# A new written order for a fused attention and highway kernel: same operations, other order, other buffers, other holds of the q loads

## The chip, the cores and the metric

The kernel runs on one core of one Trainium2 chip. The metric is the device time of one execution in microseconds (us). The core has engines that each work through their own list of instructions in order and meet only through semaphores: TensorE (PE in the profile; PEld are its weight loads), VectorE (DVE), ScalarE (ACT), GpSimd (POOL) and SyncE (SP, which here only issues DMAs). DMAs are issued from the lists of SP, POOL and (four of them) ACT, and are moved by 16 DMA engines that all of them share.

## What is computed

```python
def _attn_ref(q, k, v, tau):           # 8 batches, 12 heads, 448 tokens, 64 wide, float32
    q_n = q / (np.linalg.norm(q, axis=-1, keepdims=True) + 1e-06)
    k_n = k / (np.linalg.norm(k, axis=-1, keepdims=True) + 1e-06)
    scores = np.matmul(q_n, k_n.transpose(0, 1, 3, 2)) / tau
    scores = scores - np.max(scores, axis=-1, keepdims=True)
    attn = np.exp(scores)
    attn = attn / (np.sum(attn, axis=-1, keepdims=True) + 1e-09)
    return np.matmul(attn, v)

def _moe_ref(x, w_h, w_t, b_t):        # x: 3584 tokens x 768
    H = np.maximum(x @ w_h, 0.0)
    T = 1.0 / (1.0 + np.exp(-(x @ w_t + b_t)))
    return T * H + (1.0 - T) * x
```

The attention's output, laid out as 8 * 448 tokens by 12 * 64, is the x of the second part.

## The kernel before

**The work and its names.** Each of the 8 batches goes through the same stages. The names are those of the program's operations; the first number is mostly the batch.

- *Loads.* `ldq b` on SP; `ldk b` and `ldv4`, `ldv3` (quarters of v) on POOL, where k and v turn to 16 bits on the way. Of batch 0, q comes in three loads and k in three (`ldf 0` on ACT, `ldf 1` and `ldf 2` on SP); of batch 1, q comes in three (`ldq 1 0`, `ldq 1 1`, `ldq 1 2`). `ldwt` and `ldwh` (POOL) bring the weights, `ldb` (SP) is three loads of the bias.
- *Norms.* `sq2` squares a group of heads (ACT, some on POOL), `rd2` sums them (DVE), `ln28` and `ie28` (ACT, first two groups of batch 0 and the third) or seven `nt` steps (DVE) make one over the root, `qn7`, `kn4`, `kn3` scale (POOL, first group on DVE too).
- *Turning.* q and k are transposed either by TensorE (`tq`, `tk`, then copies `cpq`, `cpk` on DVE) or by DMA from SP (`xd7` for q from batch 3 on, `xdk` for k from batch 5 on).
- *Attention.* Six pairs of heads per batch, numbered n = 6 b + p. `qk n c` (two products of 64 rows each, L496) and `qkt n` (L507) make scores, `exp` and `expt` (ACT, L502, L509) take them to 16 bits, `av n c` and `avt n` (L521, L526, L534) multiply with v, `rc` and `ev` (DVE) divide and write x. Batch 0 is cut otherwise: `qk01`, `qt01`, `ex512`, `ex384`, `av0`.
- *Second part.* Four blocks per batch, g = 4 b + i. x is turned by DMA (`xd6 g`, `xd3 g` on SP) except in batch 0 (`xt6`, `xt3` on TensorE). `ff g wi half lo` (three products of 128 x 384, L682; `fft`, L679, for the small fourth block) are the products with wt (wi 0) and wh (wi 1). `za` (DVE) adds the bias, `th6` or `th3` (ACT) takes tanh, `gt`, `hm`, `gg` (DVE) and `out` (POOL) combine, `st g` (SP) stores. The last two blocks end in `cx`, `hg6`, `ou6`, `hg3`, `ou3` on DVE and `sl` stores on SP and ACT; the last products are two `fth`.
- *Fillers.* 57 products of zeros (`wm`, `wf`) keep TensorE working in the first 30 us.

**What sets the order.** All 1948 operations stand in one written list, `ORDER`; each engine runs its own in the order of that list. `SLOTS` gives, for each ring of buffers, which buffer the n-th tile to be touched takes (`B` are the eight PSUM banks, `qr` the two buffers of loaded q, `kr` three of k, and so on). A tile may only take a buffer whose former tile is done with, so a load also waits for the last reader of that buffer. Two further sorts of waits are put in by hand at the end of the kernel: an operation on POOL of certain kinds waits for the last one of those kinds on DVE, and the q loads of batch 1 and later (`held`) wait for whatever ACT operation stands last before them in the list. In the list before, these are: `ldq 1 0` the first table load, `ldq 1 2` an `sq1` of group 0, `ldq 1 1` `ln28 0 56`, `ldq 2` `ex384 0 1 0`, `ldq 3` `ex384 1 3 0`, `ldq 4` `th3 3`, `ldq 5` `exp 15 2 0`, `ldq 6` `exp 22 1 0`, `ldq 7` `exp 31 2 0`.

Of the kernel before, what the change touches and what calls it, by code (L numbers as in the profile page):

```python
# [94 lines left out]
""".split()  # L95
)

SLOTS = {
    "qr": "01010101",
    "kr": "0120121",  # L100
    "kn": "012012021012021021021021",
    "vr": "01010101",
    "vp": "01010101",
    "sq": "012012010201210210210210120102102100120210120210",
    "n2": "01010101",
    "y": "01201201",
    "tu": "01010101010",
# [93 lines left out]
def kernel(  # L201
# [609 lines left out]
    with nc.allow_low_precision(reason="fp16 operands of the products and gates as given"):  # L811
        with tc.manual_schedule():
            before = act = None
# [50 lines left out]
```

## Time and profile before

| | us |
|---|---|
| timed runs | 254.82, 256.25, 258.32 (median 256.25) |
| span of the profiled execution, first to last instruction | 252.9 |
| TensorE busy in it | 237.5 |
| ScalarE busy | 211.5 |
| VectorE busy | 208.0 |
| GpSimd busy | 184.0 |

The page gives no other time of the profiled execution than its span; the timed runs count what lies around it too. In the views, a line such as `L682 PE MATMUL B<-wt,xT` is an instruction of line 682 that writes a tile of ring B and reads wt and xT. Busy TensorE is not TensorE at its peak, since products overlap: a product of 384 columns counts as busy for longer than the time after which the next one may start. "From issue to landing" of a DMA counts from the start of its issuing instruction.

### The profile page before, as it was taken

The page shows a single profiled execution, that of the slowest core. Times are in us where ns is not written, and L with a number is a line of the kernel's source. Part 1 is how long each engine was busy: PE and PEld are TensorE (multiplying, and loading weights), DVE is VectorE, ACT ScalarE, POOL GpSimd, SP SyncE. Part 2 cuts the span into 40 slices and gives each one's busy share as a digit, 9 for nine tenths or more (in the row PEclk, how much of TensorE's full clock was granted, in tenths as well). Part 3 has the DMA queues.
Part 4 walks back from the last instruction along what each step waited for, and adds up shares of the span by engine and source line. Part 5 has one row for each costly group of instructions (what it writes and reads, how often), then busy time and mean ns, then how long its engine had stood idle before and what let it go on. Part 6 is the DMA issues. An engine that isn't in the chain of part 4 may idle for free.

```text
span 252.9 us, 7457 instructions
## 1 busy us (share of the span) xinstructions
PE 237.5 (94%) x2895; PEld 147.1 (58%) x2895; DVE 208.0 (82%) x462; ACT 211.5 (84%) x421; POOL 184.0 (73%) x261
## 2 busy tenths in 40 slices
PE   5959999999999999989999999999999999999990
PEld 2425776557756665645765566656656655675650
DVE  4977989999999999989899869689767665556983
ACT  3589999999999999989999999999997669981120
POOL 8369599959798979796989775878476983522540
PEclk9997999999999999999999999999999999999998
DMA  6999999999589999999999998999779588745755
GB/s 219 286 270 237 288 259 202 200 271 179 72 104 146 314 264 248 151 223 163 266 157 170 156 114 138 249 207 193 128 129 231 93 135 192 162 127 123 187 147 156
DMA packets 75892, 47.78 MB, mean 189 GB/s; under 512 B 51536, under 2 KB 72656, under 8 KB 75856
## 3 DMA queue, kind: packets, MB, share of 16 engines
q1 hardware_dynamic: 55568, 33.86, 59.2%
q0 software_dynamic: 19856, 12.68, 37.1%
q10 hardware_dynamic: 432, 0.75, 0.8%
q8 instruction: 22, 0.36, 0.6%
q14 instruction: 14, 0.11, 0.1%
HBM read 38.34 MB, written 11.01 MB: 195 GB/s over the span
## 4 chain that ended last, share of the span: by engine, by line
PE 68%; DMA 11%; ACT 8%; DVE 7%; issue 2%; POOL 2%; SPq 0%; DVEq 0%; POOLq 0%; ACTq 0%
PE B L682 26%; PE B L496 10%; PE B L526 8%; DMA xT<-x 7%; PE B L679 5%; PE B L521 3%; DMA E<-in_k_dram 3%; PE B L447 3%; ACT E L502 3%; PE B L534 3%; PE B L507 2%; PE B L573 2%; ACT sq L380 2%; PE B L305 2%; DVE hm L720 1%
## 5 line engine op out<-in xcount | busy, mean ns | idle before, releaser
L502 ACT ACTIVATE E<-B 128x448 f16<-128x448 f32 x252 | 122.8, 612 | 9.6 <-PE B L496 8.6
L682 PEld LDWEIGHTS <-xT 128*128 128x128 f16 x576 | 52.1, 98 | 39.6 <-issue 6.9
L752 POOL TENSOR_TENSOR os<-x,hm 128x384 f32<-128x384 f16 x53 | 47.6, 912 | 29.8 <-DVE hm L747 21.3
L682 PE MATMUL B<-wh,xT 128*128 128x384 f16 x288 | 56.7, 326 | 0.6 <-DMA xT<-x 0.6
L682 PE MATMUL B<-wt,xT 128*128 128x384 f16 x288 | 55.0, 326 | 1.8 <-DMA xT<-x 1.4
L432 POOL TENSOR_TENSOR kn<-kr,y 128x192 f16<-128x192 f16 (+1 forms) x84 | 45.8, 562 | 10.6 <-DVE y L409 6.1
L391 DVE TENSOR_REDUCE n<-sq 128x14 f32<-128x896 f32 (+1 forms) x50 | 51.2, 1039 | 2.8 <-ACT sq L380 2.6
L432 POOL TENSOR_TENSOR qn<-qr,y 128x448 f16<-128x448 f32 x47 | 43.9, 946 | 9.1 <-ACT y L420 4.4
L526 PE MATMUL B<-vp,E 128*128 128x65 f16 x756 | 38.7, 193 | 0.0
L724 ACT ACTIVATE tt<-z 128x768 f16<-128x768 f32 (+1 forms) x32 | 26.3, 821 | 14.6 <-DVE z L711 14.5
L720 DVE SCALAR_TENSOR_TENSOR hm<-B,x 128x384 f16<-128x384 f32 x53 | 28.8, 549 | 8.4 <-PE B L682 3.9
L526 PEld LDWEIGHTS <-E 128*128 128x128 f16 x756 | 33.7, 98 | 3.2
L496 PE MATMUL B<-qT,kT 64*128 64x448 f16 x252 | 34.8, 354 | 0.4 <-DVE hm L720 0.4
L711 DVE TENSOR_TENSOR z<-B,bias 128x384 f32<-128x384 f32 x48 | 25.8, 551 | 9.3 <-PE B L682 6.3
L521 PE MATMUL B<-vp,Et 128*128 128x130 f16 x126 | 28.1, 223 | 0.0
L380 ACT ACTIVATE sq<-qr 128x896 f32<-128x896 f32 (+1 forms) x24 | 24.1, 1022 | 3.5 <-DMA qr<-in_q_dram 3.5
L509 ACT ACTIVATE Et<-B 128x448 f16<-128x448 f32 x42 | 26.1, 631 | 0.4 <-PE B L507 0.4
L542 DVE SCALAR_TENSOR_TENSOR x<-B,rd 128x448 f16<-128x448 f32 x42 | 25.6, 618 | 0.9
L337 POOL DMA_DIRECT2D vr<-in_v_dram x32 | 21.9, 690 | 2.5 <-DVE z L711 2.5
L586 ACT ACTIVATE E<-B 128x512 f16<-128x512 f32 (+1 forms) x42 | 20.6, 607 | 0.9 <-POOL qn L432 0.5
L380 ACT ACTIVATE sq<-kr 128x896 f32<-128x896 f16 x17 | 17.0, 1041 | 1.1 <-DMA kr<-in_k_dram 1.1
L305 PE MATMUL B<-wz 128*128 128x512 f16 x39 | 14.7, 433 | 2.6 <-DVE wz L281 2.6
(81 smaller groups left out, 313.7 us busy)
## 6 DMA issues: line engine op xcount, KB each, us to landing
out_dram<-os SPq DMA_DIRECT2D x47, 192.0 KB, 3.3
qr<-in_q_dram SPq DMA_DIRECT2D x6, 1344.0 KB, 8.3
kr<-in_k_dram POOLq DMA_DIRECT2D x7, 672.0 KB, 11.6
vr<-in_v_dram POOLq DMA_DIRECT2D x16, 192.0 KB, 6.9
qr<-in_q_dram SPq DMA_DIRECT2D x6, 448.0 KB, 10.0
vr<-in_v_dram POOLq DMA_DIRECT2D x16, 144.0 KB, 7.7
out_dram<-os SPq DMA_DIRECT2D x15, 96.0 KB, 3.8
wt<-in_moe_w_t_dram POOLq DMA_DIRECT2D x1, 1152.0 KB, 24.4
```

The costliest lines, as they stand in the source:

```text
L380: nc.scalar.activation(dst, src, AF.Square, scale=sc)
L391: nc.vector.reduce_sum(R("n2", b)[:, c : c + 7 * n], a, axis=AX.X)
L432: ENG[eng].tensor_mul(N[:, :, t, :] if nm == "q" else N[:, lo > 0 : (lo > 0) + 2 * (hi - lo) - 1 : 2, t, :], source(nm, b, g)[:, t, 64 * l ...
L496: nc.tensor.matmul(R("B", ("S", n, c, t))[:, 0:S], lhsT=R("kT", i)[ln, s, 128 * c : 128 * c + 128], rhs=queries(ln), start=True, stop=True)
L502: nc.scalar.activation(R("E", n)[:, at : at + 7, :].rearrange("l j x -> l (j x)"), R("B", ("S", n, c, t))[:, 0:S], AF.Exp)
L509: op("ACT", f"expt {n}", lambda: nc.scalar.activation(R("Et", n).rearrange("l j x -> l (j x)"), R("B", ("St", n))[:, 0:S], AF.Exp), r=[("B ...
L521: nc.tensor.matmul(U[:, 2 * c : 2 * c + 2, :], lhsT=Et[:, 2 * c : 2 * c + 2, :].rearrange("l j x -> l (j x)"), rhs=vp[:, 6:8, 0:65], start ...
L526: nc.tensor.matmul(U[:, 2 * c + t, :], lhsT=E[:, at : at + 2, :].rearrange("l j x -> l (j x)"), rhs=vp[:, 3 * t + m, 0:65], start=False, s ...
L682: nc.tensor.matmul(P[:, 0:MH], lhsT=xT[:, cc, :], rhs=w_[:, cc, MH * mh : MH * mh + MH], start=(cc == 0), stop=(cc == CC - 1))
L720: op("DVE", f"hm {g} {mh}", lambda at=at, sl=sl, mh=mh: nc.vector.scalar_tensor_tensor(out=R("hm", g)[:, sl], in0=R("B", at)[:, 0:MH], sca ...
L724: op("ACT", f"th{nb} {g}", lambda: nc.scalar.activation(R("tt", g)[:, 0:W], R("z", g)[:, 0:W], AF.Tanh, scale=0.5), r=[("z", g), ("t0",)], ...
L752: op(eng, f"out {g} {mh}", lambda sl=sl, mh=mh: ENG[eng].tensor_add(R("os", g)[:, sl], xpart(mh), R("hm", g)[:, sl]), r=[("gg", g), xk], w ...
```

## The change

Operations, tiles and their sizes stay. `ORDER` and most of `SLOTS` are new, and the holds of the q loads are written out: each names the one operation that it waits for, on any engine, instead of the last ACT operation before it in the list.

```diff
@@ ORDER: all 74 lines replaced, SLOTS: most strings replaced @@
     "qr": "01010101",
     "kr": "0120121",
-    "kn": "012012012021012021021021",
-    "vr": "01010101",
+    "kn": "012012012021021021012201",
+    "vr": "01001010",
...
+HOLD = {339: 97, 340: 87, 341: 87, 578: 93, 808: 151, 1035: 228, 1262: 696, 1489: 868, 1716: 434}
...
-            before = act = None
+            before, last = None, {}
             for o in pl.ordered(ORDER, SLOTS):
                 made = len(nc.cur_bb.bb.instructions)
                 o.fn()
                 made = [i for i in nc.cur_bb.bb.instructions[made:] if i.engine == ENG[o.eng].engine]
-                if o.eng == "ACT":
-                    act = made[-1]
-                elif o.held:
-
-                    behind(made[0], act)
+                last[o.seq] = made[-1]
+                if o.seq in HOLD:
+                    behind(made[0], last[HOLD[o.seq]])
                 elif o.port and o.eng == "DVE":
                     before = made[-1]
                 elif o.port and before is not None:
```

In names, the holds are now: `ldq 1 0` behind `ln28 0 28`, `ldq 1 1` and `ldq 1 2` behind `sq2 q 0 1`, `ldq 2` behind `sq2 k 0 2`, `ldq 3` behind `ex512 1 0 0`, `ldq 4` behind `ex384 1 2 1`, `ldq 5` behind `exp 15 2 1`, `ldq 6` behind `exp 18 1 0`, `ldq 7` behind `expt 7`.

The new order in names, where the prediction speaks of it (before, then after):

```
SP, start    ldq 0 0, ldq 0 1, ldf 1, ldf 2, ldq 0 2, ldq 1 0, ldq 1 2, ldq 1 1, ldq 2, ldb, ldq 3
             ldq 0 0, ldq 0 1, ldf 1, ldq 0 2, ldf 2, ldq 1 0, ldq 1 1, ldb, ldq 1 2, ldq 2, ldq 3
POOL, start  ident, ldk 1, ldv4, ldv4, ldv3, ldv3, ldwt, qn7 ...
             ldk 1, ldv4, ldv4, ldv3, ldv3, ident, ldwt, ldv3 2 0 1, kn3 ...
ACT, start   ldf 0, table, sq1 ...
             table, ldf 0, sq1 ...
DVE, start   zvp 1, zw, zkn 1 ... rd2 q 0 1, qn7 0 0 0, zkn 0, rd2 k 0 1, kn4 0 0 0
             zw, zvp 1, zvp 0 ... rd2 q 0 1, rd2 k 0 1, qn7 0 0 0, kn3 0 0 0, kn4 0 0 0
PE, start    34 fillers, tq 0 0 ... tq 0 1, tk 0 1 (nothing between) ... tk 0 2
             37 fillers, tq 0 0 ... tq 0 1, 5 fillers, qt01, qk01, qt01, qk01, tk 0 1, tk 0 2
SP, batch 1  xd6 5, xd6 4, xd3 7, xd6 6, st 1, ldq 4
             xd6 5, xd6 4, st 0, xd3 7, ldq 4, xd6 6, st 1
SP, batch 2  xd6 10, xd6 8, xd6 9, xd3 11, st 5, st 4
             xd6 9, xd6 8, st 5, xd3 11, st 7, xd6 10
SP, batch 3  xd6 12, xd6 14, xd6 13, st 8, xd3 15
             xd6 14, xd6 12, st 2, xd6 13, xdk 5 0 1, xd3 15
SP, batch 5  st 10, xd6 20, xdk 6 2 0, xd6 22, xd7 6 2, xdk 6 2 1, xd6 21
             xdk 6 2 0, xdk 6 1 1, xdk 6 2 1, xdk 6 1 0, xd6 20, xd6 22
PE, end      ... fft 31 0, fft 31 3, ff 30 1 0 0, ff 30 1 1 3, ff 30 1 0 3, fth 31, fth 31
             ... ff 30 1 0 3, ff 30 1 1 3, fft 31 0, fft 31 3, fth 31, fth 31
```

More of the change, by code (lines that the diff above doesn't have):

```diff
@@ L100 @@
     "kr": "0120121",
-    "kn": "012012021012021021021021",
-    "vr": "01010101",
+    "kn": "012012012021021021012201",
+    "vr": "01001010",
     "vp": "01010101",
-    "sq": "012012010201210210210210120102102100120210120210",
+    "sq": "012012012012012012102102120012012201210202021201",
     "n2": "01010101",
@@ L107 @@
     "tu": "01010101010",
-    "qn": "012012012012021021021021",
-    "qT": "01230123012031203123012",
-    "kT": "01230123012301230120312",
-    "E": "012012012012012000120120120120120120120120120201201210120",
-    "Et": "012201201201201202120210210210021020102102",
-    "rd": "011001010101010101010101011010101010101010101010010101",
-    "x": "012012012",
-    "xT": "01234021340214023102401324310432",
-    "z": "01010110100101010111101001010101",
-    "tt": "01010111010101001011010001101010",
@@ L118 @@
-    "hm": "01202012201202012102201210210210",
-    "os": "01231320123023113031031020321023",
-    "B": (
-        "0123456701234567012345670123456701234567013456721061136113133524673607614250456047261353626715342610"
-        "7356421702674530153764205367162375013475103427630527605437150361724537425163401723450124351063472634"
-        "1062743501675270326175403726150361741304672510762354705462314072613546135071062573147503462152710456"
-        "3172630451634706203452706512063127043156407214031476532470615437216723507413705340127635124073156423"
-        "5017630547160423516275306473204361725014367136570425612703147352401654203521746056027451320463207456"
-        "2317354062173564037152476320417352071463207531426431507432157640317645302145630147263051"
+    "qn": "012012021021120120120201",
@@ new lines @@
+    "qT": "01230123012302103210321",
+    "kT": "01230123021302130213023",
+    "E": "012102021201012022102102102102012012012012021021020102102",
+    "Et": "012012012112021021012102012120120121201212",
+    "rd": "010101010101010101010101010101010101010101010101010101",
+    "x": "012012012",
+    "xT": "01234021340214302430124301432130",
+    "z": "01011010101010000011101101010101",
+    "tt": "01011011010110101101010110011011",
+    "hm": "01220210021201021201101210210210",
+    "os": "01230101013021323220320113210320",
@@ new lines @@
+    "B": (
+        "0123456701234567012345670123456701234567012345706324731473402436045175162753040176726042714350763410"
+        "2546071354253076013547234105264035120421675263120571354071476012765014726541350167420145726051437652"
+        "0376401657431624072136052437612735026475360213076421764013572350164752604137264052304163721530647251"
+        "0763243705420361207135247160352435761423506125457523046312507421350674513062756370461251075324176521"
+        "3046753016457301265736142326473051273402156320561274632150372654213670427062503471673120547612045162"
+        "7546541623076503217501320764536427356130426530712356147312745063274503714205176342016574"
```

149 rows, old and new, of the table ORDER are left out of this document.

## The prediction

> **What bounds the kernel now.** I read the head of the page first, then busy time by stretch, then TensorE's own waits. The fences of the stretches have as columns: the stretch, its length, busy time of PE, weight loads, DVE, ACT and POOL (instructions in brackets), granted clock, DMA share, GB/s.
>
> ```profile
> span 252.9 us, 7457 instructions
> PE 237.5 (94%) x2895; PEld 147.1 (58%) x2895; DVE 208.0 (82%) x462; ACT 211.5 (84%) x421; POOL 184.0 (73%) x261
> ```
> ```profile
> 54.00:103.00 49.00, 48.80 (x660) 31.29 (x657) 46.90 (x101) 48.88 (x102) 44.18 (x61) 1.00 0.99 191
> 103.00:150.00 47.00, 44.93 (x564) 27.13 (x561) 41.04 (x83) 45.03 (x89) 39.83 (x58) 1.00 1.11 179
> 150.00:200.00 50.00, 49.46 (x605) 31.35 (x602) 40.09 (x90) 46.42 (x97) 36.52 (x52) 1.00 0.99 178
> 200.00:240.00 40.00, 40.00 (x452) 24.76 (x449) 26.77 (x62) 24.16 (x51) 20.43 (x26) 1.00 0.68 146
> ```
>
> Averages hide the stages here. From 54 to 103 us TensorE (48.80 of 49 us) and ScalarE (48.88) are both full, and each paces the other: no order of the same work shortens that stretch by more than the 0.2 us that is idle. From 103 to 150 both lose about 2 us. From 150 on ScalarE has slack, and after 200 TensorE alone is full. So the end is set by: when the full stretch begins, what TensorE waits for between 103 and 200, and the few us after its last matmul.
>
> TensorE's waits in all (engine, line, waited for: us, times, longest):
>
> ```profile
> PE B L447 <- POOL kn L432: 2.5, 1, 2.5
> PE B L682 <- DMA xT<-x: 2.0, 2, 1.4
> PE B L496 <- DVE hm L720: 0.4, 1, 0.4
> ```
>
> The first is in the start, the other two in the middle. The timeline shows the middle ones in place (start, length, what; in brackets idle time of the arrays and who ended it):
>
> ```profile
> 106.64 0.35 PE L507 MATMUL B<-qT,kT 128*128 128x448 f16 x1
> 108.43 1.15 PE L682 MATMUL B<-wt,xT 128*128 128x384 f16 x6 [1.45 <-DMA xT<-x]
> ...
> 139.81 0.35 PE L507 MATMUL B<-qT,kT 128*128 128x448 f16 x1
> 140.00 0.65 PE L682 MATMUL B<-wt,xT 128*128 128x384 f16 x3
> ...
> 141.45 0.66 PE L682 MATMUL B<-wh,xT 128*128 128x384 f16 x3 [0.56 <-DMA xT<-x]
> ```
>
> An L507 product lets the next instruction begin 0.19 us after it (139.81 to 140.00). At 106.64 it took 1.79 us, so that wait costs 1.6 us; the second costs 0.6, the one on DVE 0.4. What did they wait for? The chain of waits names two transposes of x by DMA, and the views of their lines give time from issue to landing:
>
> ```profile
> 100.76 7.62 DMA xT<-x
> 130.47 10.94 DMA xT<-x
> ```
> ```profile
> L662 SPq DMA_TRANSPOSE xT<-x x1: 1211/1211/1211, 98.1 to 98.1; - x1
> DMA to landing us min/median/max: 3.3/3.3/3.3
> ```
> ```profile
> L322 POOL DMA_DIRECT2D kr<-in_k_dram x1: 845/845/845, 101.2 to 101.2; - x1
> DMA to landing us min/median/max: 11.1/11.1/11.1
> ```
>
> A transpose issued at 98.1 lands in 3.3 us. The one issued at 100.76 takes 7.6: at 101.2 GpSimd issues the 672 KB load of k 6, which itself takes 11.1. The one at 130.47 takes 10.9, just after the load of k 7. So a transpose that meets a k load is 4 to 8 us late, and the before order puts the first consumer right there.
>
> **The change, part by part.** No instruction is added or removed; 2895 matmuls, 462 DVE operations and so on stay. Counted in both orders, TensorE changes between kinds of tiling (full, two row halves, two column halves) 184 times before and 183 after, so its work without waits is the same to 0.1 us. All that can change is waiting and the tail.
>
> *Middle: minus 2.6.* In batch 2 the new SP order is xd6 9, xd6 8, st 5, xd3 11, st 7, xd6 10; before it was xd6 10, xd6 8, xd6 9. How long TensorE works between the last products of a batch and the first use of its transposes I counted from the new order, at 0.49 us for a group of three matmuls of ff:
>
> ```profile
> 228.44 10.85 PE B L682 x66
> ```
>
> (66 in 10.85) and likewise for the others. ff 9 comes some 7 us after them; being first, its transpose should land within about 5 (some 1.7 from the products to the issue, as now, and 3.3 to land). The 1.6 goes. In batch 3 the order is xd6 14, xd6 12, st 2, xd6 13, and ff 13 still comes 14 us after the products: the late one has the same room, but xd6 14 is wanted 5.8 us after them, with 0.5 to spare. I take the 0.6 as gone and keep 0 as the other end. The 0.4 on DVE's hm is a matter of which PSUM bank comes free; with new banks it is gone or elsewhere: taken as gone. Price if the cover fails: a k load issued 2 us earlier against these transposes brings back 1.6 and 0.6 and, by the row of 130.47, up to 6 more.
>
> *Start: plus 1.7 (from minus 1.5 to plus 4.3).* This is the part with the widest bounds.
>
> ```profile
> 16.70:19.30 2.60, 0.08 (x2) 0.00 (x0) 2.50 (x3) 2.60 (x6) 1.57 (x4) 1.00 1.43 221
> 19.30:22.80 3.50, 3.48 (x22) 1.99 (x23) 2.34 (x3) 2.98 (x7) 3.50 (x6) 0.51 1.21 227
> ...
> 27.00:54.00 27.00, 26.51 (x404) 17.35 (x401) 24.83 (x65) 26.71 (x54) 22.62 (x33) 1.00 1.25 238
> ```
>
> Now TensorE stands 2.5 us for the k transpose of group 1, then runs 3.5 us at clock 0.51. The new order puts five fillers and four small score groups between tq 0 1 and tk 0 1, which covers this wait. But ScalarE was full then (2.60 of 2.60), and it leads into the full stretch; what TensorE gains only helps if ScalarE comes sooner too. ScalarE meets a new wait:
>
> ```profile
> 25.37 0.97 ACT L380 ACTIVATE sq<-qr 128x896 f32<-128x896 f32 x1
> ```
> ```profile
> L324 SPq DMA_DIRECT2D qr<-in_q_dram x1: 367/367/367, 7.2 to 7.2; - x1
> DMA to landing us min/median/max: 11.6/11.6/11.6
> ```
> ```profile
> L324 SPq DMA_DIRECT2D qr<-in_q_dram x1: 368/368/368, 18.1 to 18.1; - x1
> DMA to landing us min/median/max: 8.4/8.4/8.4
> ```
> ```profile
> L322 SPq DMA_DIRECT2D qr<-in_q_dram x1: 368/368/368, 21.5 to 21.5; - x1
> DMA to landing us min/median/max: 12.6/12.6/12.6
> ```
> ```profile
> L349 SPq DMA_DIRECT2D biast<-in_moe_b_t_dram x2: 582/787/992, 22.6 to 23.2; - x2
> DMA to landing us min/median/max: 14.5/14.7/14.8
> ```
>
> SP's loads of batch 1 are now q 1 0, q 1 1, the three bias loads, q 1 2. At present the second q load of batch 1 lands at 18.8 (7.2 plus 11.6), and the bias loads, behind q 2 (landed 34.1), are done by 38.0 (23.2 plus 14.8): they took 3.9 us. In the new order q 1 2 waits behind them: 18.8 plus 3.9, plus its own 448 KB. Seven loads of this size left SP's queue between 0.74 and 18.8, 2.6 each; the next took 8.4 from its issue at 18.1, while the weights came. With 2.6 for q 1 2 it lands at 25.3, with 5.9 at 28.6 (the 8.4 count from the issue; a load that already stands in the queue spares the way to its first packet, by estimate about one interval of that pace); I take 3.3, since the weights still come: 26.0. On ScalarE sq2 q 1 2 moves ahead of three exponentials (ex512 1 0 0, ex512 1 0 1, ex384 1 0 1), about 1.4 us, so ScalarE comes to it at 24.0 where it now starts at 25.37, and everything behind it on ScalarE (the exponentials of groups 1 and 2, so their PSUM banks and TensorE) waits 1.3 to 4.6, with 26.0 two. The lateness at the same place of its work is the same figure: it starts 0.6 later and has 1.4 more to do. Of that, the 0.3 that it idles now between 27 and 54 comes back: 1.0 to 4.3, and 1.7 taken, the value nearest to the rows of the early loads. Below nothing: if the bias is quicker than here and the covered 2.5 us bring ScalarE forward, a gain of up to 1.5.
>
> The first fillers run out before the first transpose: 37 stand ahead of tq 0 0 (34 now), but VectorE's reduction of k group 1 now goes ahead of its scaling of q group 0:
>
> ```profile
> 11.08 1.08 DVE L391 TENSOR_REDUCE n<-sq 128x14 f32<-128x896 f32 x1 [0.36 <-ACT sq L380]
> ```
> ```profile
> 11.45 0.55 PE L447 MATMUL B<-ident,qn 128*128 128x128 f16 x7
> ```
>
> The scaling, one operation of about 1 us, then starts at 12.2, and tq 0 0 moves from 11.45 to about 13.2. By the rows above an idle of 2.5 us was followed by 3.5 us at clock 0.51, so a slow stretch is likely there too; TensorE has little but fillers then, and it costs nothing while ScalarE is the later.
> The Trainium skill, TensorE: Matmul & The Clock Gate, section Why this matters for your kernels, lets gaps of up to about 3 us pass without a slower clock. The trace disagrees: 2.6 us of idle sufficed. By that page the stretch would run at full clock, and the sum would be the same.
>
> *Holds of the q loads: nothing, 0 to plus 1.* q 3 to q 5 are freed earlier and then wait for their buffer, or stand behind xd3 7 and st 0. If st 0 holds SP's queue (it waits for GpSimd's out 0 0, and ldq 4 0, xd6 6, st 1 stand behind), ScalarE waits up to 1 us in its full stretch. q 7 is wanted some 4 us earlier by ScalarE and issued no earlier; ScalarE had 3.6 us idle between 150 and 200, which covers it.
>
> *Queues: SP's batch 6.* Four key transposes, about 1.25 us each to issue, now stand ahead of xd6 20, and they wait for GpSimd's scaling, which runs later in the new order. Taken as covered, 0; plus 2 if not.
>
> *Tail: plus 0.4.* After the last attention both orders have 38 groups of products. But fft 31 now comes last but two, three groups (1.5 us) later than now:
>
> ```profile
> 244.07 0.55 DVE L711 TENSOR_TENSOR z<-B,biast 128x384 f32<-128x384 f32 x1
> 245.34 1.02 DVE L714 SCALAR_TENSOR_TENSOR hm<-B,tt 128x384 f16<-128x384 f32 x2 [0.72 <-POOL os L752]
> ...
> 246.45 1.02 DVE L717 TENSOR_TENSOR os<-hm,os 128x384 f32<-128x384 f16 x2
> 247.39 0.35 DVE L699 SCALAR_TENSOR_TENSOR hm<-B,tt 128x192 f16<-128x192 f32 x1
> ...
> 248.39 0.61 DVE L702 TENSOR_TENSOR os<-hm,os 128x192 f32<-128x192 f16 x2
> ```
>
> Now z of group 31 is made while TensorE still works; in the new order z (0.55) stands in DVE's closing chain and the two L714 ahead of it, the second half of which (0.5) closes the chain now. The rest is the same, but L726 waits for ScalarE's tanh of that z (about 0.5), which L717 covers only in part: 0.4 longer, between 0.1 and 0.5.
>
> Sum: 1.7 - 1.6 - 0.6 - 0.4 + 0.4 = -0.5 us. The profiled span becomes 252.4. That execution has no other time on the page; the timed runs' median, 256.25, lies 3.35 above its span (lowest run 1.9). On the median: **255.7**, which is no change that can be measured.
>
> **Rivals.** *(a) Slower: ScalarE's wait for q 1 2 sets everything.* If the bias and q 1 2 land at 28.6, ScalarE enters the full stretch 4.3 late, with the tail 4.7; of the 2.6 in the middle only the last two waits come back (0.6 and 0.4), since ScalarE is still the later engine at 106. Plus 3.7: 260. It decides from a landing past 27 us (then the start costs more than the 2.6 of the middle). For it: the 8.4 us row. Against it: the early loads' pace. *(b) Everything goes well.* The start gains the 2.5 us wait and the half-clock time (3.5 us at 0.51, 1.7): minus 4.2, and the middle minus 2.6, tail plus 0.4: minus 6.4, 249.9. Against it: ScalarE is full from 16.7 on. *(c) It doesn't do what it says.* Transposes still meet a k load, only other ones, and the waits move: start 0, middle 0, tail 0.4: 256.7. For it: xd6 14 with its 0.5 us to spare, and the k loads, which are as large as now.
>
> **How the numbers follow.** Forecast 0.45, (a) 0.2, (b) 0.15, (c) 0.2. The forecast alone spans 253.5 to 258; (a) and (b) stretch the range to 250.2 and 260.8, which also takes up the 3.5 us between lowest and highest of the three runs. A measurement of this kernel tells about 2% (5.1 us) from no change: faster by that needs (b) nearly whole, 0.15; slower needs (a) with a second wait such as SP's batch 6, 0.12; within it 0.73.
>
> **What would show it.** Right: no xT wait of over 0.5 us between 100 and 145; no wait at tk 0 1; ScalarE waiting 2 us for qr near 24 to 26; a closing chain on DVE that is some 0.4 longer. Wrong: ScalarE's wait absent or over 4 us; a transpose of 8 us or more that TensorE waits for; key transposes of batch 6 with TensorE idle; TensorE's 54 to 103 stretch no longer full.

## The result, and the profile after

The changed kernel is slower: a median of 263.3 us beside 255.5 for the kernel before, and a ratio of 1.035 (95% interval 1.026 to 1.044). Runs that are over 1.5% slower than the fastest of their kernel are left out of this ratio and of all those below, so it is not the quotient of the two medians. Forecast were 255.7 and at most 260.8. The profiled execution's span is 259.8 where it was 252.9, 6.9 us more. Line numbers are 4 higher than before, and in the experiments they shift by a line or two. First the head of the page and the stretches of the changed kernel (columns as in the prediction):

```profile
span 259.8 us, 7459 instructions
...
PE 241.7 (93%) x2895; PEld 147.1 (57%) x2895; DVE 209.8 (81%) x462; ACT 213.3 (82%) x421; POOL 186.8 (72%) x261
```
```profile
29.30:33.50 4.20, 4.12 (x44) 2.63 (x44) 2.63 (x5) 3.67 (x8) 2.53 (x3) 0.50 1.16 293
54.00:103.00 49.00, 48.45 (x671) 29.89 (x666) 45.95 (x98) 48.01 (x99) 43.52 (x59) 1.00 0.99 186
103.00:150.00 47.00, 45.54 (x534) 27.33 (x532) 43.30 (x90) 45.49 (x91) 40.46 (x59) 1.00 1.10 178
```

The counts of operations are those of before, as they should be. The full stretch from 54 on is still full for TensorE, but ScalarE, which had 48.88 of 49 us there, now has 48.01: it stands for 1.0 us. TensorE's waits of the changed kernel, then ScalarE's and TensorE's own timelines where the longest wait lies:

```profile
PE B L601 <- ACT E L590: 5.0, 1, 5.0
...
PE B L686 <- DMA xT<-x: 1.2, 1, 1.2
...
PE B L500 <- DVE z L715: 0.6, 1, 0.6
```
```profile
27.89 0.95 ACT L384 ACTIVATE sq<-qr 128x896 f32<-128x896 f32 x1 [4.89 <-DMA qr<-in_q_dram]
```
```profile
29.38 0.29 PE L601 MATMUL B<-vp,E 128*128 128x130 f16 x1 [4.99 <-ACT E L590]
```

The long wait is the one that the prediction had looked for, ScalarE at the square of q 1 2 (L384), but it lasts 4.89 us and not 2. TensorE waits 4.99 behind it, and its granted clock then stays at 0.50 for 5.0 us, up to 34.4 (the first row of the stretches shows 4.2 of them). Why 4.89? The loads on SP's queue, time from issue to landing (q 1 1, the last two of the three bias loads, q 1 2):

```profile
L328 SPq DMA_DIRECT2D qr<-in_q_dram x1: 471/471/471, 12.5 to 12.5; - x1
DMA to landing us min/median/max: 7.6/7.6/7.6
```
```profile
L353 SPq DMA_DIRECT2D biast<-in_moe_b_t_dram x2: 582/584/585, 13.5 to 14.2; - x2
...
DMA to landing us min/median/max: 10.3/10.4/10.5
```
```profile
L328 SPq DMA_DIRECT2D qr<-in_q_dram x1: 586/586/586, 14.8 to 14.8; - x1
...
DMA to landing us min/median/max: 13.0/13.0/13.0
```

q 1 1 is there at 20.1, the bias at 24.5 and q 1 2 at 27.8. Two things differ from the prediction's sum: q 1 1 comes 1.3 later than the 18.8 that I had carried over (its batch is held behind `ln28 0 28` and was issued from 12.09 on, so that the queue, done with its older loads at 14.4, had a gap: by the trace's DMA packets it sent almost nothing from 13.9 to 15.8), and ScalarE is at this square at 23.0, not at 24.0.

In the middle, the wait for a transpose at 106 is gone, and one of 1.2 has come at 147.8. There the transpose xd6 13 was issued at 136.9, just behind the load of k 7:

```profile
L326 POOL DMA_DIRECT2D kr<-in_k_dram x1: 900/900/900, 136.0 to 136.0; - x1
...
DMA to landing us min/median/max: 11.5/11.5/11.5
```
```profile
L666 SPq DMA_TRANSPOSE xT<-x x1: 1454/1454/1454, 136.9 to 136.9; - x1
...
DMA to landing us min/median/max: 10.8/10.8/10.8
```

Load and transpose land together, at 147.5 and 147.7. At the end, the last products of TensorE (first the kernel before, then the changed one):

```profile
245.28 1.18 PE L695 MATMUL B<-wh,xT 128*64 128x192 f16 x24
```
```profile
251.65 1.16 PE L699 MATMUL B<-wh,xT 128*64 128x192 f16 x24
```

They end 6.3 us later, so the tail behind them takes the other 0.6. Since the work is the same, lateness at any point is the time there less the work that lies ahead of it in that kernel's order; counted so for TensorE it is 5.2 us at 30 to 34 us. So of the 6.9, about 5.2 come from the start, 1.1 from the middle and 0.6 from the tail.

### The profile page after: what moved, and what is told of

Same layout as the page of the kernel before. It is cut to its first block, busy times and chain, and to the rows that moved or that the text cites. A ratio compares the mean times of both kernels' runs of the same rounds, so it can differ in the third digit from the quotient of the medians.

```text
span 259.8 us, 7459 instructions
## 1 busy us (share of the span) xinstructions
PE 241.7 (93%) x2895; PEld 147.1 (57%) x2895; DVE 209.8 (81%) x462; ACT 213.3 (82%) x421; POOL 186.8 (72%) x261
## 5 line engine op out<-in xcount | busy, mean ns | idle before, releaser
L756 POOL TENSOR_TENSOR os<-x,hm 128x384 f32<-128x384 f16 x53 | 48.9, 933 | 32.2 <-DVE hm L751 24.2
L686 PE MATMUL B<-wt,xT 128*128 128x384 f16 x288 | 56.3, 326 | 1.2 <-DMA xT<-x 1.2
L436 POOL TENSOR_TENSOR kn<-kr,y 128x192 f16<-128x192 f16 (+1 forms) x84 | 46.4, 570 | 14.5 <-DVE hm L751 5.6
L728 ACT ACTIVATE tt<-z 128x768 f16<-128x768 f32 (+1 forms) x32 | 25.2, 798 | 16.7 <-DVE z L715 16.6
L500 PE MATMUL B<-qT,kT 64*128 64x448 f16 x252 | 36.8, 354 | 1.6 <-DVE z L715 0.6
L384 ACT ACTIVATE sq<-qr 128x896 f32<-128x896 f32 (+1 forms) x24 | 23.5, 992 | 9.0 <-DMA qr<-in_q_dram 8.3
L513 ACT ACTIVATE Et<-B 128x448 f16<-128x448 f32 x42 | 24.9, 608 | 2.6 <-PE B L511 1.5
L590 ACT ACTIVATE E<-B 128x384 f16<-128x384 f32 (+1 forms) x42 | 20.2, 572 | 1.0 <-PE B L577 0.7
L500 PEld LDWEIGHTS <-kT 64*128 64x128 f16 x252 | 9.3, 94 | 15.8 <-issue 11.9
L384 ACT ACTIVATE sq<-kr 128x896 f32<-128x896 f16 x17 | 16.8, 1028 | 0.5 <-DVE n L395 0.5
```

Of the source, the lines that this page charges most:

```text
L384: nc.scalar.activation(dst, src, AF.Square, scale=sc)
L436: ENG[eng].tensor_mul(N[:, :, t, :] if nm == "q" else N[:, lo > 0 : (lo > 0) + 2 * (hi - lo) - 1 : 2, t, :], source(nm, b, g)[:, t, 64 * l ...
L500: nc.tensor.matmul(R("B", ("S", n, c, t))[:, 0:S], lhsT=R("kT", i)[ln, s, 128 * c : 128 * c + 128], rhs=queries(ln), start=True, stop=True)
L686: nc.tensor.matmul(P[:, 0:MH], lhsT=xT[:, cc, :], rhs=w_[:, cc, MH * mh : MH * mh + MH], start=(cc == 0), stop=(cc == CC - 1))
L756: op(eng, f"out {g} {mh}", lambda sl=sl, mh=mh: ENG[eng].tensor_add(R("os", g)[:, sl], xpart(mh), R("hm", g)[:, sl]), r=[("gg", g), xk], w ...
```

## The experiments

Kernels with the same order can be compared product by product. The two tables give the start of the same product in us, against the kernel that was edited (its own time in the first column); they are worked out from the traces, one profiled execution of each kernel (ff 30 is its product `ff 30 1 1 3`). The ratios are to the kernel before, timed beside each of the changed ones, with a 95% interval.

```
product   changed | bias behind | no holds | both | weights late | k 7 later | still later | k 5 square
qk 7 2     47.7   |   -5.1      |  -5.3    | -5.7 |    -3.2      |   -5.7    |   -5.8      |  -5.8
qk 12 0    73.5   |   -5.1      |  -5.4    | -5.7 |    -3.2      |   -5.7    |   -5.8      |  -5.8
qk 23 2   124.6   |   -4.8      |  -5.1    | -5.4 |    -3.8      |   -5.4    |   -5.5      |  -5.6
qk 27 0   143.6   |   -4.8      |  -5.0    | -5.4 |    -3.8      |   -5.4    |   -5.5      |  -5.5
qk 30 0   160.0   |   -2.0      |  -4.4    | -1.9 |    -3.2      |   -5.9    |   -5.3      |  -6.0
ff 30     250.1   |   -1.8      |  -4.2    | -1.6 |    -3.3      |   -5.5    |   -4.2      |  -4.6

product   before  | bias ahead | x 9 first | all three | k loads later | and bias ahead
qk 7 2     40.2   |   -0.9     |  -0.3     |   -0.3    |    -0.5       |    -0.2
qk 12 0    68.2   |   -0.8     |  -0.3     |   -0.3    |    -0.5       |    -0.2
qk 23 2   119.2   |   +2.1     |  +6.4     |   +4.0    |    -1.3       |    -1.5
ff 30     244.2   |   +1.3     |  +6.5     |   +4.6    |    -0.9       |    -0.7
```

**The start, first four kernels.** *The bias behind q 1 2.*

```diff
 SP:  ldq 1 0, ldq 1 1,
-     ldb, ldq 1 2, ldq 2
+     ldq 1 2, ldb, ldq 2
```

> The changed kernel, with one entry of the order moved: on SP's queue the three bias loads stand behind the load of q 1 2 instead of ahead of it. First theory (the bias is what makes q 1 2 late): q 1 2 lands one load after q 1 1, at 20.1 + 3.3 = 23.4 us instead of 27.8; ScalarE, at that square at 23.0, waits 0.4 to 0.7 instead of 4.9; 4 to 4.5 us come back, span 255.3 to 255.8 against 259.8. Second theory (the hold of q 1 0 is the cause, since it left the queue idle from 14.4 to about 16): that idle time is still there, q 1 2 lands at about 27 and the span stays above 259. Third theory (TensorE is the bound and the start is made up for by the waits in the middle): the wait goes, but less than 2 us of the span.

Ratio to before 1.013 (1.005 to 1.020). ScalarE's timeline at the square:

```profile
24.25 0.95 ACT L382 ACTIVATE sq<-qr 128x896 f32<-128x896 f32 x1 [1.46 <-DMA qr<-in_q_dram]
```

The start comes 5.1 earlier. But the wait is 1.46 and not 0.4 to 0.7: q 1 2, now directly behind q 1 1 (19.9), took until 24.2, 4.3 us for 448 KB, where q 1 1 ahead of it had taken 1.9. So the bias isn't all: something slows the queue after 20 us.

*No holds in batch 1.*

```diff
-HOLD = {339: 97, 340: 87, 341: 87, 578: 93, ...}
+HOLD = {578: 93, ...}
```

> The changed kernel without the three holds of batch 1 (q 1 0, q 1 1, q 1 2); bias still ahead of q 1 2. First theory (bias): the queue runs on from 14.4 without the gap of about 1.6 us, so everything behind lands that much earlier, q 1 2 at about 26.2; ScalarE's wait falls from 4.9 to about 3.3; span about 258.2. Second theory (holds): the wait is gone or under 1 us, span 255 to 256. A side effect that would speak for the holds: the k and weight loads, which share the queues, land later.

1.012 (1.001 to 1.022).

```profile
23.40 0.95 ACT L382 ACTIVATE sq<-qr 128x896 f32<-128x896 f32 x1 [0.61 <-DMA qr<-in_q_dram]
```

With the bias still ahead of it, q 1 2 lands at 23.3: the wait is down to 0.61 all the same, as the second theory had it and the first hadn't. The bias pieces now land at 21.2, 2.9 us after q 1 1, and q 1 2 takes 2.1.

*The kernel before with the bias early.*

```diff
 SP:  ldq 1 0, ldq 1 2,
-     ldq 1 1, ldq 2, ldb
+     ldb, ldq 1 1, ldq 2
```

> The kernel before, with one entry of the order moved: the three bias loads stand ahead of the last q load of batch 1 (there it is q 1 1) instead of behind q 2. First theory (bias): q 1 1 lands later by the bias pieces' 4 us, at about 30.5 instead of 26.5; ScalarE comes to its square at 27.1 and waits about 3; span 252.9 + 3 = 256. By the second theory (holds) nothing changes: within 0.5 us of the kernel before.

0.998 (0.993 to 1.003), and no wait of 3: the last q load lands at 26.4 as before (17.6 plus 8.7), and ScalarE loses 0.54 (the view names VectorE, but the square begins 0.1 behind the landing):

```profile
L323 SPq DMA_DIRECT2D qr<-in_q_dram x1: 374/374/374, 17.6 to 17.6; - x1
...
DMA to landing us min/median/max: 8.7/8.7/8.7
```
```profile
26.47 0.95 ACT L379 ACTIVATE sq<-qr 128x896 f32<-128x896 f32 x1 [0.54 <-DVE vp L467]
```

The bias moved between 18.4 and 20.7, in a time when that queue has nothing else (q 1 1 is held until 17.6). Where the queue would stand idle anyway, the bias costs nothing: my first theory, that the bias as such is the cause, falls here. (The 2.1 us that the table shows for it at qk 23 2 came at ff 9, where TensorE waited 2.1 us and then had clock 0.50 for 3.4.)

*Both edits in the changed kernel.*

```diff
 SP:  ldq 1 0, ldq 1 1,
-     ldb, ldq 1 2, ldq 2
+     ldq 1 2, ldb, ldq 2
-HOLD = {339: 97, 340: 87, 341: 87, 578: 93, ...}
+HOLD = {578: 93, ...}
```

> The changed kernel with both edits: bias behind q 1 2, and no holds in batch 1. First theory (bias): nothing beyond what the moved bias alone gives, or at most the last 0.4 to 0.7 us of the wait: span 254.8 to 255.8, still 2 to 3 above the kernel before, because of waits in the middle of the changed order. Second theory (holds): clearly faster than the moved bias alone, by 2 or more. Third (middle): the start's offset is that of the kernel before, and the time is still above it by the 2 us that TensorE loses between 91 and 155.

1.014 (1.006 to 1.021). ScalarE doesn't wait at all at this square (22.53, at once), q 1 2 landed at 20.1. The start is 5.7 earlier, 0.3 to 0.6 more than by either edit alone. Either alone brings nearly all.

**What slows SP's queue after 20 us?** A new theory: it shares the engines with GpSimd's queue, whose weight load comes behind its four small v loads. *The weights later.*

```diff
 POOL: ident,
-      ldwt, ldv3 2 0 1, ..., ldwh
+      ldv3 2 0 1, ..., ldwt, ldwh
```

> The changed kernel, start not mended, with GpSimd's load of the first weight (wt) moved behind the small v load, just ahead of the second (wh), at about 22 us instead of 5.5. First theory (q 1 2 is late because from about 20 us on SP's queue shares the engines with the weight load): with only v loads beside it the bias takes about 2.3 and q 1 2 about 2.0 us, landing at 24.4 instead of 27.8; ScalarE's wait falls from 4.9 to about 1.4, and 3.5 us come back, as far as the weights are there when the first ff product wants them at about 38 to 41 (if they land at 40, nothing is lost; each us beyond costs one). Rival (bias and q 1 2 take 4.4 and 3.3 in any company, the queue's order and its gap alone decide): q 1 2 lands at 27.8 again, and the time is that of the changed kernel, 1.035 of before.

1.020 (1.011 to 1.029), beside 1.035 (1.026 to 1.044) without the edit; the two intervals just overlap. q 1 2 was issued at 15.0 and landed at 25.3; the wait is 2.12:

```profile
25.37 0.95 ACT L382 ACTIVATE sq<-qr 128x896 f32<-128x896 f32 x1 [2.12 <-DMA qr<-in_q_dram]
```

Holds and bias are as in the changed kernel, yet the bias takes 2.4 us instead of 4.4 and q 1 2 takes 2.5 instead of 3.3. So the neighbour on the other queue sets the pace. The DMA packets in the traces show it directly. In the changed kernel SP's queue moved 177 GB/s from 20 to 22 us and 129 from 22 to 27, while GpSimd's moved 107 and 129; with the weights later SP's moved 257 and 294, beside 51 and 9. The hold feeds the same mechanism: while SP's queue has its gap, GpSimd's moves on. Its fourth v quarter, issued at 4.2, lands 17.9 us later with the hold (first kernel: changed) and 20.6 without (second: no holds), and the first packet of the weight load goes at 19.5 with it and at 22.7 without:

```profile
L341 POOL DMA_DIRECT2D vr<-in_v_dram x1: 697/697/697, 4.2 to 4.2; - x1
DMA to landing us min/median/max: 17.9/17.9/17.9
```
```profile
L339 POOL DMA_DIRECT2D vr<-in_v_dram x1: 697/697/697, 4.2 to 4.2; - x1
DMA to landing us min/median/max: 20.6/20.6/20.6
```

So the lost 5 us need three things together: the bias ahead of q 1 2, the hold, and the weight load beside them. With any one of them taken away, 3.2 to 5.3 us come back.

**The middle.** With both edits 3.4 us of the gain were lost again at ff 13, between qk 27 0 and qk 30 0 in the table (with the moved bias alone 2.8, without the holds alone 0.6). That kernel there, TensorE's timeline and the stretches around it:

```profile
143.82 1.14 PE L684 MATMUL B<-wt,xT 128*128 128x384 f16 x3 [2.62 <-DMA xT<-x]
```
```profile
140.00:143.80 3.80, 1.20 (x19) 0.50 (x15) 2.11 (x5) 3.31 (x7) 3.71 (x6) 0.89 1.46 60
143.80:149.00 5.20, 5.18 (x29) 2.65 (x31) 2.22 (x6) 1.00 (x2) 0.79 (x1) 0.50 1.16 245
```

xd6 13 was issued at 131.4, 0.8 behind the load of k 7, and landed 12.4 later with it. The 2.62 us of waiting are followed by 6.0 us at clock 0.50 (to 149.8; the second row shows 5.2 of them), which cost nearly as much again. *k 7 loaded later* (on top of both edits):

```diff
 POOL: kn3 5 0 0,
-      ldk 7, kn4 5 0 0, out 8 1, kn3 5 0 1, ...
+      kn4 5 0 0, out 8 1, kn3 5 0 1, ldk 7, ...
```

> The changed kernel with the start mended (no holds in batch 1, bias behind q 1 2), and GpSimd's load of k 7 three operations later in its order (behind the scaling kn3 5 0 1 instead of ahead of kn4 5 0 0), so that SP's transpose xd6 13 is issued some 2 us ahead of it and no longer just behind it. Theory (a transpose that is issued just behind a k load lands only with that load): xd6 13 lands in 3 to 4 us instead of 12.4, TensorE's wait of 2.7 at ff 13 goes and with it the slow clock behind it, 5 us in all: span 253.4 against 258.4 without this edit. Rival (the wait only moves on): the key transposes of batch 5 and xd3 15 now meet the load and come after 148, TensorE waits there instead; gain under 1.5 us. Rival (xd6 13 is late for its place behind st 2, not for the k load): it lands late as before, gain 0.

1.010 (1.004 to 1.016); span 254.4.

```profile
L664 SPq DMA_TRANSPOSE xT<-x x1: 1302/1302/1302, 131.4 to 131.4; - x1
...
DMA to landing us min/median/max: 3.3/3.3/3.3
```
```profile
L324 POOL DMA_DIRECT2D kr<-in_k_dram x1: 900/900/900, 133.0 to 133.0; - x1
...
DMA to landing us min/median/max: 7.6/7.6/7.6
```

The transpose, issued at the same time, lands in 3.3 instead of 12.4, and the load itself takes 7.6 instead of 13.0. The wait at ff 13 and the slow clock are gone, 4.0 us between the two profiled spans. The timed medians show less, 259.0 and 257.0 (taken in two sessions), and the two ratios overlap, so the gain in time isn't clear of noise. One reason may be that the wait is not always so dear: in the five traces of the changed order in which xd6 13 is late it is 1.2 to 2.7 us, and only the two over 2.6 were followed by a slow clock. No run shows how it varies for one kernel. About 1 us of the gain goes at qk 31 0. I put that down to xdk 5 0 1, which now stands behind the load; the trace says otherwise. That transpose had landed at 141.1, qk 31 1 had read its tile at 148.7, and what ends the wait is a PSUM bank that VectorE frees, as in the changed kernel (0.61 there):

```profile
149.89 0.36 PE L498 MATMUL B<-qT,kT 64*128 64x448 f16 x2 [0.79 <-DVE z L713]
```

*The kernel before with xd6 9 first,* the step to which the prediction gave 1.6 us.

```diff
 SP:
-     xd6 10, xd6 8, xd6 9, xd3 11
+     xd6 9, xd6 10, xd6 8, xd3 11
```

> The kernel before with one entry of the order moved: the transpose xd6 9 is issued ahead of xd6 10 and xd6 8, so that it is first of its batch, as in the changed order (it keeps its buffer). My reading of the middle (what counts is which transpose meets the k load): the wait of 1.6 at ff 9 goes, and as xd6 8 and xd6 10 have other places to go late, nothing else comes: span 251.3, 0.6% faster. Rival (the load of k 6 catches whichever transpose is third, and xd6 8 or xd6 10 is now wanted as early): the wait moves to ff 8 or ff 10, gain 0 to 0.5.

Slower, 1.017 (1.008 to 1.025). xd6 9 itself lands in 3.0 us. But xd6 8 is third now, issued at 101.0 just behind the load of k 6 (100.8), and lands with it, and ff 8 comes sooner than ff 9:

```profile
L661 SPq DMA_TRANSPOSE xT<-x x1: 1292/1292/1292, 101.0 to 101.0; - x1
...
DMA to landing us min/median/max: 9.8/9.8/9.8
```
```profile
110.84 1.14 PE L681 MATMUL B<-wt,xT 128*128 128x384 f16 x3 [5.62 <-DMA xT<-x]
```

The profiled execution took 261.1 us and the fastest of this kernel 257.0, so this wait may be at the long end. Being first clears a transpose, then, and hands its place beside the load to another. In the changed kernel the load of k 6 had moved too: it was issued at 109.7, some 5 us behind xd6 9 (104.8, landed in 2.8), and met none of the transposes that are wanted soon:

```profile
L666 SPq DMA_TRANSPOSE xT<-x x1: 1212/1212/1212, 104.8 to 104.8; - x1
...
DMA to landing us min/median/max: 2.8/2.8/2.8
```
```profile
L326 POOL DMA_DIRECT2D kr<-in_k_dram x1: 891/891/891, 109.7 to 109.7; - x1
```

*With the bias ahead and k 7 behind kn3 5 0 1 as well:*

```diff
 SP:   ldq 1 0, ldq 1 2,
-      ldq 1 1, ldq 2, ldb
+      ldb, ldq 1 1, ldq 2
...
-      xd6 10, xd6 8, xd6 9
+      xd6 9, xd6 10, xd6 8
 POOL:
-      ldk 7, out 8 0, kn3 5 0 0, out 8 1, kn3 5 0 1
+      out 8 0, kn3 5 0 0, out 8 1, kn3 5 0 1, ldk 7
```

> The kernel before with three entries of the order moved: bias loads ahead of its last q load of batch 1, xd6 9 first of its batch, and k 7 loaded behind the scaling kn3 5 0 1 (some 3 us later). If the gains add up: start minus 0.9 (as the moved bias alone showed), 1.6 at ff 9 (2.3 in the run with the moved bias), 0.6 at ff 13: span 249.8 to 250.4, 1 to 1.2% faster than before. If the stretch from 54 to 103 us is set by ScalarE's work alone, the 0.9 stays and the others too, as they lie behind it. Rival (waits move on): within 0.5% of before.

1.016 (1.008 to 1.024), for the same reason: TensorE waits 4.2 at ff 8.

*The kernel before, only the k loads moved* (and two squares of ScalarE that read them).

```diff
 POOL:
-     ldk 6, kn4 4 0 0, qn7 4 0 1, kn4 4 1 0, kn3 4 2 1
+     kn4 4 0 0, qn7 4 0 1, kn4 4 1 0, kn3 4 2 1, ldk 6
...
-     ldk 7, out 8 0, kn3 5 0 0, out 8 1
+     out 8 0, kn3 5 0 0, out 8 1, ldk 7
 ACT: sq2 k 6 2 later, to just ahead of sq2 k 6 1; sq2 k 7 2 later, to just ahead of sq2 k 7 0
```

> The kernel before, transposes in their old order, but GpSimd's two k loads that meet them later in its order: k 6 behind the scaling kn3 4 2 1 (at about 104.8 us instead of 101.2), k 7 behind out 8 1 (at about 132 instead of 129.6); ScalarE's squares of k 6 2 and k 7 2, which would now wait for these loads, stand just ahead of its next square of the same k. Theory (a transpose that is issued less than about 0.5 us ahead of a k load, or behind it, lands only with the load; 1 us ahead is enough to be clear): xd6 9 lands in 3 to 4 us instead of 7.6, xd6 13 likewise instead of 10.9; the waits of 1.6 at ff 9 and 0.7 at ff 13 go: span 250.6, minus 0.9%. Rival (the loads then catch the next transposes, xd3 11 and the key transposes of batch 5, and the waits move there): gain below 0.5, or a loss.

0.997 (0.994 to 1.000), span 251.9. xd6 13 lands in 2.9 us instead of 10.9, xd6 9 in 5.8 instead of 7.6 (3 to 4 were expected):

```profile
L661 SPq DMA_TRANSPOSE xT<-x x1: 1322/1322/1322, 129.2 to 129.2; - x1
DMA to landing us min/median/max: 2.9/2.9/2.9
```
```profile
103.00:150.00 47.00, 46.67 (x595) 28.85 (x592) 42.84 (x88) 45.98 (x91) 41.94 (x60) 1.00 1.08 180
```

TensorE has 46.67 of the 47 us in this stretch, where it had 44.93. No wait for a transpose is left in its list. Counted product by product as in the table, 1.6 us are gained at ff 9 and 0.7 at ff 13; about 1.4 is given back in small waits behind them. *The same, and the bias ahead:*

```diff
 SP:  ldq 1 0, ldq 1 2,
-     ldq 1 1, ldq 2, ldb
+     ldb, ldq 1 1, ldq 2
```

> The same, and the three bias loads ahead of the last q load of batch 1 on SP's queue. The moved bias alone brought the middle forward by 0.8 at 50 to 88 us and 0.2 to 0.3 at 98 to 106. If what was gained at the start stays: span 250.0 to 250.4. If the stretch that is full on both engines eats it: as the kernel with the later k loads alone, within 0.3 us.

0.9945 (0.991 to 0.998), span 252.2. The two can't be told apart (median 253.9 both), so what the bias adds stays open; this is the one version whose interval lies clear of both kernels, 0.2 to 0.9% faster than before. That is small, and the same median without the bias edit isn't clear of no change.

**What is left of the changed order's loss,** 1.0% with the start mended and k 7 later. The start is no part of it: it was 5.2 us late and is 5.7 earlier now, about 0.5 ahead of the kernel before. So some 2 us are lost behind it, 0.6 of them in the tail. *k 7 later still:*

```diff
 POOL: kn3 5 0 1,
-      ldk 7, out 8 0, ..., ldv3 5 0 1
+      out 8 0, ..., ldv3 5 0 1, ldk 7
```

> The changed kernel with the start mended, and k 7 loaded later still: behind the small v load ldv3 5 0 1, at about 139 us, instead of 133. There the key transpose xdk 5 0 1 and xd3 15 are out ahead of it too. Theory (as above): the wait of 0.97 at qk 31 0, which came when xdk 5 0 1 was caught by the load, goes as well: span 253.4 against 254.4. Rival (the next key transposes and q transposes of batch 5 are caught, and ScalarE's square of k 7 2 waits for the load): 254.4 or more.

1.011 (1.004 to 1.018), no better. The rival was right: xdk 5 0 1 is clear, but the next transposes of batch 5 are behind the load (138.6). The key transpose issued at 140.2 takes 9.1 us, the q transpose of 143.4 takes 6.9, to 150.2, and for this one TensorE stands 1.6 at qk 31 1:

```profile
150.28 0.55 PE L498 MATMUL B<-qT,kT 64*128 64x448 f16 x4 [1.64 <-DMA qT<-qn]
```

*The square of k 5 0 behind the next exponentials (five of them; the expectation counts four):*

```diff
 ACT:
-     sq2 k 5 0, th6 5, exp 15 1 1, exp 15 2 0, exp 16 1 0, exp 16 2 1, exp 16 1 1
+     th6 5, exp 15 1 1, exp 15 2 0, exp 16 1 0, exp 16 2 1, exp 16 1 1, sq2 k 5 0
```

> The changed kernel with the start mended and k 7 three operations later, and ScalarE's square of k 5 0 four exponentials later in its order (behind exp 16 1 1 instead of ahead of exp 15 1 1). In the run without this edit ScalarE stood 0.90 us at that square for VectorE's reduction of the tile before it in the same buffer, the exponentials behind it came late, and TensorE waited 0.9 for a PSUM bank (second product of qk 16 2). Theory (the new order of ScalarE put the square ahead of its buffer, and in the stretch where both engines are full such a wait is paid in full): both waits go, span 253.5 against 254.4, time 0.4% shorter, which leaves some 0.6% to the kernel before. Rival (the square then stands ahead of the next exponentials, and the bank wait moves to groups 16 and 17): within 0.3 us of the kernel without the edit.

1.011 (1.005 to 1.016): no gain. ScalarE's wait at the square (first row, without the edit) goes, and one for TensorE's scores comes in its place (second row, with it):

```profile
84.83 0.95 ACT L382 ACTIVATE sq<-kr 128x896 f32<-128x896 f16 x1 [0.90 <-DVE n L393]
```
```profile
86.21 0.98 ACT L504 ACTIVATE E<-B 128x448 f16<-128x448 f32 x2 [0.79 <-PE B L498]
```

What makes up this last 1% is not settled. Behind the start, TensorE's views show only waits of 0.2 to 0.8 us, most of them for PSUM banks, and the two edits against such waits gave nothing: with one TensorE waits for another transpose, with the other ScalarE waits for scores.

## Why the prediction was wrong

- **What bounds the kernel: right.** With both engines full from 54 us on, a start that is 5.1 to 5.7 us earlier stays that much earlier up to 73 us (the first two rows of the table are the same within 0.1), and nothing absorbs it.
- **The start, plus 1.7: the wrong step, by 3.5.** It measured 5.2. The mechanism was the named one (the wait at q 1 2) and rival (a) had its form, with a landing past 27; the wait was mis-sized, 4.89 us and not 2. The landing was taken at 26.0 and was 27.8, since the new hold of q 1 0 was not counted as a gap in the queue (1.3) and the bias was 0.5 slower; q 1 2 itself took 3.3, as assumed and for the reason given, the weights. ScalarE was there 1.0 sooner; I had counted its time as fixed. That lengthens the wait but makes nothing later. Behind the wait comes what the sum had no term for: TensorE's clock is at 0.50 up to 34.4, and ScalarE stands another 1.0 us there for products (first 0.69, then 0.27):

```profile
33.71 0.49 ACT L590 ACTIVATE E<-B 128x384 f16<-128x384 f32 x1 [0.69 <-PE B L577]
```

The landing's 1.8 and this 1.0 make 2.8 of the 3.5, and the 0.3 that was to come back did not. I had "the early loads' pace" against rival (a); that pace ends where the weight load begins, at 19.5 us.
- **The middle, minus 2.6: wrong by 3.7.** That the wait at 106 goes came true (no wait for xT between 100 and 145), but for another reason than "being first, its transpose should land within about 5": the k load had moved. That reason holds for the one transpose (3.0 us), but tried by itself it made the middle 6.7 us later in the profiled execution (1.7% in the timed ones), at ff 8, since the load then caught xd6 8. The 0.6 at 140 didn't go; it became 1.2 at 147.8, with xd6 13 once more behind the load of k 7. The prediction's "by the row of 130.47, up to 6 more" saw the danger and priced it at nothing in the sum; I looked at the place of a transpose among transposes, and not at its place against the k load on GpSimd's list. And new waits for PSUM banks came, about a microsecond near 91 to 97 and others behind; "with new banks it is gone or elsewhere" was priced at minus 0.4 only.
- **tk 0 1:** covered, as forecast (no wait for POOL kn of more than 0.2). What it is worth can't be seen here, since ScalarE came later.
- **tq 0 0** was forecast at 13.2 and came at 12.4. **The holds of q 3 to q 7 and SP's batch 6:** no wait that I could put down to them.
- **The tail, plus 0.4:** 0.6 by the ends of TensorE, a little over its bounds of 0.1 to 0.5.
- **Chances.** What came is (a) at the start and (c), transposes that meet a k load in another place, in the middle. They were given chances as if only one could come. The two errors had the same sign, and the range let rival (a) come with the gains of the middle nearly whole. With the middle at zero, as its rows of 7.6 and 10.9 allowed, (a) alone gives 256.25 + 4.3 + 0.4 = 261.

## What to carry to other kernels

Price a load that moves behind others by what runs on the other queue at the time at which it will move, and not by the pace of an earlier stretch; a hold that leaves a queue idle gives that time to its neighbour and is paid twice. When a transpose by DMA is late, look at which large load was issued close to it, on any engine's list, and move the load: here, reordering the transposes only chose the victim. Where two engines were full, whatever the start lost stayed lost, and the two small waits that were taken away there came back elsewhere.

## What the runs showed of the hardware that I had not expected

- Transposes and k loads hold each other up. Issued 1.6 us ahead of the load, a transpose landed in 3.3 us and the load in 7.6; issued 0.8 behind it, the transpose took 12.4, the load 13.0, and all DMA together moved only 60 GB/s from 140.0 to 143.8, beside 245 right after. One issued 1.1 ahead (99.7 against 100.8, xd6 9 first) took 4.4. At leads of 0.4 to 0.5 in the kernel before, xd6 9 took 7.6 (100.76 against 101.22) and xd6 14 took 5.1, so the lead isn't all. Other loads do it as well: xd6 6 took 10.0 in the changed kernel, issued 0.6 behind the load of q 4 on its own queue.
- The same 448 KB on SP's queue took 1.9 to 2.1 us before the weight load began and 3.3 to 4.3 beside it, while the bias loads took between 2.3 and 4.4. Where both queues had work, the trace has about as many packets of one as of the other, so that each queue's share went with the size of its packets. In the changed kernel these were 422 and 425 from 16 to 19 us, mostly 1792 bytes on SP's queue and 384 on GpSimd's (252 and 54 GB/s), and 371 and 421 from 22 to 27, with 1536 on GpSimd's (129 each).
- TensorE's waits of 2.62 and 4.99 us were followed by 6.0 and 5.0 us at clock 0.50; the one of 1.19 was not (the three products behind it take 0.66, the usual time). In between both came: 1.79 us in the kernel with only the k loads moved and 1.78 with the weights later were followed by 3.4 us at 0.50, while 1.78 at ff 13 without the holds was not.

```profile
147.76 0.66 PE L686 MATMUL B<-wt,xT 128*128 128x384 f16 x3 [1.19 <-DMA xT<-x]
```
